# Another hand-written order for the attention stage, and the 1e-9 of the softmax sums added on another engine

## The chip, the cores and the metric

The kernel runs on one core of a Trainium2 chip. The metric is the device time of one execution in microseconds. A core has five engines that take their instructions in the order in which the program queues them, each from a queue of its own: TensorE (PE; its weight loads are PEld), VectorE (DVE), ScalarE (ACT), GpSimd (POOL) and SyncE (SP), which here only issues DMAs. They wait for each other through semaphores.

## What is computed

Causal attention over 2 batches of 12 heads (448 positions, 64 columns a head), then two mixer blocks on the 2 x 448 x 768 result. All of it is in float32 precision; weights come as 64-bit floats and are converted on the chip.

```python
def _attn_ref(q, k, v):
    scores = scale * np.matmul(q, k.transpose(0, 1, 3, 2))
    mask = np.triu(np.ones((seq, seq), dtype=bool), k=1)
    scores = np.where(mask, -1000000000.0, scores)
    scores = scores - np.max(scores, axis=-1, keepdims=True)
    attn = np.exp(scores)
    attn = attn / (np.sum(attn, axis=-1, keepdims=True) + 1e-09)
    return np.matmul(attn, v).astype(np.float32)

def _moe_ref(x, w_tok1, w_tok2, w_ch1, w_ch2):
    h = np.maximum(xt @ w_tok1, 0.0) @ w_tok2       # xt: x with positions last
    u = x + h.transpose(0, 2, 1)
    return u + np.maximum(u @ w_ch1, 0.0) @ w_ch2
...
def _moe2_ref(x, w_ch1, w_ch2):
    u = x + np.real(np.fft.fft(np.fft.fft(x, axis=1), axis=2))
    un = (u - mean(u)) / np.sqrt(var(u) + 1e-06)
    return u + np.maximum(un @ w_ch1, 0.0) @ w_ch2
```

## The kernel before

The heads are worked on in 12 pairs, n = 0 to 11, two heads side by side in TensorE's rows. The attention stage is written as a list of words, the string ORDER. A loop at the end of the stage calls one small function for each word, in the order of the list, and inside `tc.manual_schedule` this is also the order in which each engine's queue receives its instructions. So the list fixes, for every engine, what stands behind what; what can be ready when is left to the semaphores.

The words of a pair n, with the engine in brackets: Kn and Vn load q and k, and v (SyncE issues the DMAs; only the k of pair 0 is issued by ScalarE, in two halves, in `load_k`). Sn.g are the scores (TensorE), in three groups, g = 0 for the blocks of 112 and 224 columns, 1 for 336 and 2 for 448; pair 0 has four groups. Nn.i adds the mask and takes the negated maxima (VectorE, line 328, two instructions and two accumulator reads), and gives the PSUM bank of the block back. En.i is the exponential with its sum (ScalarE, line 338). Tn.u transposes the probabilities (TensorE, line 351, five groups of four), Cn.u copies them to SBUF (u = 1 and 3 on ScalarE, the others on VectorE, line 358). Pn multiplies with v (TensorE, line 371), On copies the result (ScalarE). Zn makes the divisors out of the sums: `divisors`, two instructions on VectorE, lines 385 and 386. Xn transposes back (TensorE, line 392), xn divides (VectorE, line 405), hn and gn split the result into a high and a low part (ScalarE, GpSimd).

Between them stand the words of the first mixer's start: A, B, D (TensorE) with r, s, b, d, u, w around them on ScalarE, VectorE and GpSimd; Rk loads the raw words of a weight, and Wk.0 to Wk.5 convert them (ScalarE, three times VectorE, ScalarE, GpSimd); U, Y are the first matmuls with converted weights, y, z, a what follows them. The word I0 is `tables`: an exponential on one column of a small tile, so that ScalarE's table is loaded early, and a memset of 1e-6 on VectorE over that column (lines 202 and 203).

PSUM has eight banks, given out in turn by `grab` and put back into the ring by `drop`; a word that takes a bank waits for the last reader of the bank's earlier use. SBUF tiles have few buffers too: two for v, two for each parity of pairs for q and k, two for raw weights. Behind the stage the rest of the program goes on with matmuls whose order the change doesn't touch.

Of the kernel before, what the change touches and what calls it, by code (L numbers as in the profile page):

```python
# [10 lines left out]
F32 = mybir.dt.float32  # L11
# [4 lines left out]
AF = mybir.ActivationFunctionType  # L16
ALU = mybir.AluOpType
# [4 lines left out]
TS = 112  # L22
# [48 lines left out]
ENGINES = {getattr(mybir.EngineType, e) for e in ("PE", "DVE", "Activation", "Pool", "SP")}  # L71


ORDER = """K0 I0 S0.1 S0.0 K1 S0.2 N0.1 K2 N0.0 S0.3 E0.1 N0.2 S1.0 E0.0 S1.1 N0.3 V0 K3 N1.1 E0.2 N1.0 E0.3 S1.2 T0.2 N1.2
E1.1 V1 C0.2 K4 N1.3 T0.4 T0.0 E1.0 R0 T0.1 T0.3 E1.2 C0.0 S2.1 C0.1 C0.4 S2.0 C0.3 S2.2 E1.3 P0 N2.2 Z0 N2.0
T1.1 N2.1 E2.2 E2.1 O0 T1.2 Z1 T1.0 T1.4 E2.0 N2.3 C1.2 C1.0 E2.3 C1.4 V3 X0 T1.3 x0 S3.0 S3.1 C1.1 Z2 N3.1 S3.2
W0.0 C1.3 N3.0 K5 P1 E3.0 N3.2 T2.0 E3.2 O1 E3.1 T2.2 W0.1 C2.0 T2.1 T2.3 X1 T2.4 B0.0 C2.1 C2.2 N3.3 C2.3 S4.1
b0.0 x1 S4.2 h0 C2.4 E3.3 V2 N4.2 S4.0 P2 T3.2 E4.2 T3.4 N4.3 N4.1 T3.0 W0.2 N4.0 E4.3 R1 g0 K6 W0.3 O2 V5 T3.3
E4.1 X2 T3.1 C3.0 E4.0 C3.4 x2 T4.2 C3.1 T4.0 S5.1 C3.3 C3.2 h2 N5.2 P3 W0.4 E5.2 S5.0 O3 N5.0 C4.0 C4.2 S5.2 g2
B0.2 h1 T4.4 W1.0 T4.3 W0.5 N5.1 N5.3 b0.2 T4.1 C4.1 g1 K7 A0.0 B0.1 C4.4 W1.1 A0.1 R2 V4 C4.3 Z4 E5.0 E5.3 W1.2  # L80
E5.1 Z3 r0.0 b0.1 X3 r0.1 P4 S6.0 O4 S6.1 W1.3 s0.0 W1.4 x3 T5.3 Z5 T5.2 N6.1 T5.1 s0.1 N6.0 C5.3 W1.5 T5.4 C5.2
T5.0 E6.0 C5.1 E6.1 X4 N6.2 C5.0 D0.1 K8 x4 V6 S6.2 E6.2 R3 S7.0 C5.4 W2.0 N6.3 N7.1 S7.1 h4 P5 E6.3 N7.2 V7
D0.0 B1.1 E7.2 T6.4 K9 d0.1 E7.1 O5 T6.0 W2.1 b1.1 g4 X5 T6.2 D0.2 N7.0 C6.0 C6.4 E7.0 x5 d0.0 W3.0 T6.3 T6.1 h5
C6.3 d0.2 C6.2 S7.2 S8.0 S8.1 g5 N7.3 C6.1 h3 N8.0 N8.2 S8.2 N8.1 E7.3 N8.3 g3 P6 T7.3 Z7 E8.2 E8.3 W3.1 T7.0
W2.2 B1.0 C7.3 K10 u0.2 C7.0 W2.3 T7.2 A1.1 Z6 W3.2 T7.4 T7.1 O6 E8.1 A1.0 b1.0 W2.4 B1.2 C7.1 C7.2 C7.4 X6 r1.0
P7 r1.1 s1.0 S9.2 E8.0 b1.2 S9.0 R4 s1.1 O7 x6 S9.1 u0.0 N9.3 h6 T8.4 X7 N9.2 E9.3 N9.1 V8 D1.0 E9.2 x7 V9 C8.4
T8.3 T8.0 T8.2 d1.0 C8.2 N9.0 C8.0 W3.3 K11 g6 T8.1 u1.0 C8.1 w0.2 C8.3 S10.0 u0.1 w1.0 S10.2 E9.1 N10.1 N10.3
P8 N10.0 E9.0 T9.4 T9.2 W3.4 D1.1 Z8 C9.2 O8 E10.3 T9.0 V11 w0.0 E10.1 T9.3 E10.0 D1.2 X8 h7 T9.1 C9.3 d1.1 C9.4
C9.0 d1.2 S11.2 S11.0 W2.5 x8 u1.1 h8 S10.1 N11.3 C9.1 S11.1 N11.0 E11.3 g7 N10.2 E10.2 P9 T10.1 N11.2 T10.0
N11.1 T10.3 E11.0 V10 E11.1 E11.2 C10.3 C10.0 g8 T10.2 Z9 T10.4 w1.1 C10.4 R5 Z10 A2.0 C10.2 C10.1 P10 W3.5  # L90
T11.4 w0.1 O9 T11.2 W4.0 W4.1 T11.0 T11.1 C11.4 O10 u1.2 W5.0 T11.3 W4.2 C11.3 C11.0 C11.1 A2.1 r2.0 C11.2 P11
X9 B2.1 X10 w1.2 W5.1 W4.3 B2.0 r2.1 B2.2 s2.0 s2.1 b2.1 D2.0 x9 R6 W4.4 x10 W5.2 D2.1 W5.3 O11 W4.5 W5.4 Z11 U2
y2 h10 X11 h9 D2.2 z2 b2.0 d2.1 R7 g10 W5.5 x11 d2.0 U0 W6.0 h11 W6.1 B3.0 g11 b3.0 g9 U3 A3.0 y0 y3 A3.1 r3.0
B3.2 b3.2 W6.2 z0 r3.1 s3.0 W7.0 W6.3 s3.1 U1 u2.0 W6.4 D3.1 b2.2 B3.1 D3.0 b3.1 y1 W7.1 W7.2 D3.2 W7.3 u2.1
W6.5 w2.0 W7.4 z1 z3 W7.5 d3.1 d2.2 d3.0 u3.1 w3.1 d3.2 Y0 u2.2 Y1 u3.2 w2.1 u3.0 a0 w3.0 w2.2 a1 w3.2
"""


# [5 lines left out]
def fused_kernel(ctx: ExitStack, tc: tile.TileContext, qk, v, w1, w2, wa, wb, wc, wd, fa, fb, out):  # L104
    nc = tc.nc
    mm = nc.tensor.matmul
    vec, act, pool = nc.vector, nc.scalar, nc.gpsimd

    const = ctx.enter_context(tc.tile_pool(name="const", bufs=1))
# [9 lines left out]
    vec.memset(mean_w, 1.0 / DM)  # L119
    ones = const.tile([1, 16], F32, name="ones")  # L120
    vec.memset(ones, 1.0)
    eps_t = const.tile([128, 16], F32, name="eps_t")[:, :1]

    resid = [[res.tile([128, S], F32, name=f"resid{ct}_{b}") for b in range(B)] for ct in range(NCT)]
    act_h = [[res.tile([128, S], F32R, name=f"acth{ct}_{b}") for b in range(B)] for ct in range(NCT)]
# [143 lines left out]
    with ExitStack() as actx:  # L269
        ap = actx.enter_context(tc.tile_pool(name="attn", bufs=2))  # L270
        a1 = actx.enter_context(tc.tile_pool(name="attn1", bufs=1))
# [4 lines left out]
            out=mask[:, S - TS :], in_=mask[:, S - TS :], pattern=[[-1, TS]], compare_op=ALU.is_ge, fill=MASKED,  # L276
# [105 lines left out]

        def divisors(n):
            c = pairs[n]
            vec.scalar_tensor_tensor(out=c.ssum, in0=c.ssum, scalar=1.0e-9, in1=c.ssum, op0=ALU.add, op1=ALU.max)
            vec.reciprocal(out=c.ssum, in_=c.ssum)

        def rows(n):
# [104 lines left out]
        raw, ahead, g0 = {}, [None] * (len(sources) - 2), {}  # L493
# [25 lines left out]
        def early_add(x):  # L519
# [3 lines left out]
        ops = dict(  # L523
            I=tables, K=load_k, V=load_v, S=scores, N=maxima, E=exps, T=transposes,
            C=pt_copy, P=pv, O=pv_copy, Z=divisors, X=rows, x=divide, h=x_high, g=x_low, A=mix_in, r=mix_high,
            s=mix_low, B=channels, b=channels_copy, D=mix_out, d=mix_add, u=split_high, w=split_low, R=load_raw,
            W=convert_part, U=lambda k: early_up(k, 0), y=lambda k: early_up(k, 1), z=lambda k: early_up(k, 2),
            Y=early_down, a=early_add,
        )
        with tc.manual_schedule(engines=ENGINES):  # L530
            for word in ORDER.split():
                ops[word[0]](*[int(x) for x in word[1:].split(".")])
# [274 lines left out]
    inv, rstd, g2, pools = {}, [], {}, {}  # L807
# [77 lines left out]
    with tc.manual_schedule(engines=ENGINES):  # L885
        for word in ORDER2.split():
            name = word.rstrip("0123456789.")
# [99 lines left out]
```

## Time and profile before

| | |
|---|---|
| median of 3 runs | 673.29 us (673.22 to 673.49) |
| the profiled execution | 673.2 us, of which the span is 671.4 us |
| busy share of the span | TensorE 99%, weight loads 91%, VectorE 79%, ScalarE 42%, GpSimd 17% |
| granted TensorE clock | 0.999 of full speed over the span |
| attention stage | from the start to 139.2 us |

The page gives the busy time of each engine; a matmul's end is modelled, and matmuls overlap, so a short wait of TensorE can be hidden in what is shown as busy. The chain of waits is followed back from the last instruction, and each of its pieces ends where the next one starts: there the lengths of groups of the same work can be compared. The timeline gives single instructions with their start, the windows the busy time in a stretch.

### The profile page before, as it was taken

The page shows a single profiled execution, that of the slowest core. Times are in us where ns is not written, and L with a number is a line of the kernel's source. Part 1 is how long each engine was busy: PE and PEld are TensorE (multiplying, and loading weights), DVE is VectorE, ACT ScalarE, POOL GpSimd, SP SyncE. Part 2 cuts the span into 40 slices and gives each one's busy share as a digit, 9 for nine tenths or more (in the row PEclk, how much of TensorE's full clock was granted, in tenths as well). Part 3 has the DMA queues.
Part 4 walks back from the last instruction along what each step waited for, and adds up shares of the span by engine and source line. Part 5 has one row for each costly group of instructions (what it writes and reads, how often), then busy time and mean ns, then how long its engine had stood idle before and what let it go on. Part 6 is the DMA issues. An engine that isn't in the chain of part 4 may idle for free.

```text
span 671.4 us, 10118 instructions
## 1 busy us (share of the span) xinstructions
PE 665.5 (99%) x3838; PEld 610.6 (91%) x3838; DVE 533.7 (79%) x1016; ACT 282.9 (42%) x601; POOL 111.2 (17%) x86
## 2 busy tenths in 40 slices
PE   9999999999999999999999999999999999999997
PEld 6787889999999999999999999999999999999996
DVE  7988877688988955899899869988868898556751
ACT  7989784433333333335564422224332324232200
POOL 0042343310000000400510008261002320000000
PEclk9999999999999999999999999999999999999999
DMA  7532221184352331200233232333332434222311
GB/s 230 199 133 73 106 80 63 67 253 157 136 179 95 126 109 48 95 1 1 96 113 138 97 125 94 142 99 137 105 116 102 150 142 142 82 76 76 118 42 55
DMA packets 21541, 73.77 MB, mean 110 GB/s; under 512 B 2850, under 2 KB 7714, under 8 KB 21124
## 3 DMA queue, kind: packets, MB, share of 16 engines
q1 hardware_dynamic: 20628, 69.64, 29.9%
q0 software_dynamic: 576, 3.25, 1.5%
q8 instruction: 30, 0.49, 0.3%
q10 hardware_dynamic: 288, 0.23, 0.1%
q14 instruction: 19, 0.16, 0.1%
HBM read 70.36 MB, written 2.75 MB: 109 GB/s over the span
## 4 chain that ended last, share of the span: by engine, by line
PE 96%; DVE 3%; DMA 1%; ACT 0%; SPq 0%; issue 0%
PE psum L234 13%; PE psum L236 13%; PE psum L235 13%; PE psum L255 13%; PE psum L260 13%; PE psum L259 12%; PE psum L351 4%; PE psum L315 4%; PE psum L371 3%; PE psum L441 3%; PE psum L475 2%; PE psum L746 1%; PE psum L392 1%; PE psum L461 1%; PE psum L677 1%; DMA k<-in_qk 1%
## 5 line engine op out<-in xcount | busy, mean ns | idle before, releaser
L255 PE MATMUL psum<-gh,wh 128*128 128x448 f32 x432 | 157.3, 364 | 0.0
L234 PE MATMUL psum<-acth,wh 128*128 128x448 f32 x432 | 156.8, 363 | 0.0
L236 PE MATMUL psum<-actl,wh 128*128 128x448 f32 x432 | 156.6, 363 | 0.0
L260 PE MATMUL psum<-gl,wh 128*128 128x448 f32 x432 | 156.6, 362 | 0.0
L235 PE MATMUL psum<-acth,wl 128*128 128x448 f32 x432 | 155.8, 361 | 0.0
L259 PE MATMUL psum<-gh,wl 128*128 128x448 f32 x432 | 155.7, 360 | 0.0
L142 ACT ACTIVATE m<-w 128x512 f32<-128x512 f32 (+2 forms) x92 | 70.9, 772 | 119.8 <-DVE wl L162 82.0
L160 ACT CAST wh<-m 128x512 fp32r<-128x512 f32 (+1 forms) x90 | 63.4, 704 | 92.5 <-PE psum L260 53.5
L260 PEld LDWEIGHTS psum<-gl,wh 128*128 128x128 f32 x432 | 81.1, 188 | 6.2
L236 PEld LDWEIGHTS psum<-actl,wh 128*128 128x128 f32 x432 | 81.1, 188 | 5.9
L235 PEld LDWEIGHTS psum<-acth,wl 128*128 128x128 f32 x432 | 80.9, 187 | 5.8
L259 PEld LDWEIGHTS psum<-gh,wl 128*128 128x128 f32 x432 | 80.8, 187 | 5.8 <-issue 0.2
L255 PEld LDWEIGHTS psum<-gh,wh 128*128 128x128 f32 x432 | 81.1, 188 | 4.6 <-issue 0.2
L234 PEld LDWEIGHTS psum<-acth,wh 128*128 128x128 f32 x432 | 81.0, 188 | 4.6
L149 DVE SCALAR_TENSOR_TENSOR m<-w,m 128x512 uint32<-128x512 uint32 (+2 forms) x92 | 80.2, 872 | 2.3
L162 DVE TENSOR_TENSOR wl<-m,wh 128x512 fp32r<-128x512 f32 (+1 forms) x84 | 69.4, 829 | 15.0 <-ACT wh L160 14.6
L153 DVE SCALAR_TENSOR_TENSOR m<-w,m 128x512 uint32<-128x512 uint32 (+2 forms) x92 | 79.1, 861 | 2.0
L144 DVE TENSOR_SCALAR m<-m 128x512 f32<-128x512 f32 (+2 forms) x92 | 51.0, 554 | 31.2 <-ACT m L142 30.9
L240 ACT ACTIVATE gh<-psum 128x448 fp32r<-128x448 f32 x72 | 37.8, 540 | 71.0 <-PE psum L236 70.7
L242 DVE SCALAR_TENSOR_TENSOR gl<-psum,gh 128x448 fp32r<-128x448 f32 x72 | 43.6, 618 | 30.2 <-ACT gh L240 30.2
L145 DVE TENSOR_SCALAR m<-m 128x512 uint32<-128x512 uint32 (+2 forms) x92 | 48.9, 532 | 2.4
L338 ACT ACTIVATE p<-p,small 112x224 f32<-112x224 f32 (+3 forms) x96 | 49.6, 519 | 3.0 <-DVE small L328 2.9
(144 smaller groups left out, 741.7 us busy)
## 6 DMA issues: line engine op xcount, KB each, us to landing
w<-in_wc SPq DMA_DIRECT2D x24, 768.0 KB, 4.3
w<-in_wd SPq DMA_DIRECT2D x36, 512.0 KB, 3.2
w<-in_wa SPq DMA_DIRECT2D x12, 768.0 KB, 4.4
w<-in_wb SPq DMA_DIRECT2D x18, 512.0 KB, 3.2
v<-in_v SPq DMA_DIRECT2D x12, 256.0 KB, 2.6
out<-t SPq DMA_DIRECT2D x12, 224.0 KB, 1.9
q<-in_qk SPq DMA_DIRECT2D x11, 224.0 KB, 3.8
k<-in_qk SPq DMA_DIRECT2D x11, 224.0 KB, 3.6
```

The source lines that it names most:

```text
L142: act.activation(out=m, in_=hi.bitcast(F32), func=AF.Abs)
L144: vec.tensor_scalar(out=m, in0=m, scalar1=F64_MIN, scalar2=F64_MAX, op0=ALU.max, op1=ALU.min)
L149: vec.scalar_tensor_tensor(out=mu, in0=lo, scalar=29, in1=mu, op0=ALU.logical_shift_right, op1=ALU.bitwise_or)
L153: vec.scalar_tensor_tensor(out=mu, in0=hi, scalar=0xC0000000, in1=mu, op0=ALU.bitwise_and, op1=ALU.bitwise_or)
L160: act.copy(wh, m)
L162: low_engine[0].tensor_tensor(out=wl, in0=m, in1=f(wh), op=ALU.subtract)
L234: mm(pb[:, :S], lhsT=lh, rhs=act_h[ct][b], start=ct == 0, stop=False)
L235: mm(pb[:, :S], lhsT=ll, rhs=act_h[ct][b], start=False, stop=False)
L236: tail[0] = mm(pb[:, :S], lhsT=lh, rhs=act_l[ct][b], start=False, stop=ct == NCT - 1).ins
L255: mm(pb[:, :S], lhsT=lh, rhs=gh, start=j + k == 0 and seeded is None, stop=False, skip_group_check=seeded is not None,)
L259: mm(pb[:, :S], lhsT=ll, rhs=gh, start=False, stop=False, skip_group_check=seeded is not None)
L260: tail[0] = mm(pb[:, :S], lhsT=lh, rhs=gl, start=False, stop=j == last and k == nk - 1, skip_group_check=seeded is not None,).ins
```

## The change

Three things change. The list ORDER has the same words in another order; the order within each engine's queue changes with it. The 1e-9 is added to the sums by an activation (Identity with a bias) on ScalarE, and only the reciprocal stays on VectorE. The tile that held the 1e-6 has a second column, set to 1e-9 at the start, for this bias.

Of the order, these parts are spoken of below: the beginning (I0 now stands ahead of K0, and the scores of pair 1 begin with S1.2), the loads V5, R1, V4 behind P3, and the words around S7.2 and S9.2.

```diff
-ORDER = """K0 I0 S0.1 S0.0 K1 S0.2 N0.1 K2 N0.0 S0.3 E0.1 N0.2 S1.0 E0.0 S1.1 N0.3 V0 K3 N1.1 E0.2 N1.0 E0.3 S1.2 T0.2 N1.2
-E1.1 V1 C0.2 K4 N1.3 T0.4 T0.0 E1.0 R0 T0.1 T0.3 E1.2 C0.0 S2.1 C0.1 C0.4 S2.0 C0.3 S2.2 E1.3 P0 N2.2 Z0 N2.0
...
+ORDER = """I0 K0 S0.1 S0.0 S0.2 K1 N0.1 S0.3 E0.1 N0.0 V0 N0.2 S1.2 N0.3 E0.0 S1.0 S1.1 E0.2 K2 E0.3 N1.0 N1.3 V1 T0.2 E1.3
+T0.0 T0.1 N1.1 T0.3 C0.2 T0.4 C0.1 N1.2 C0.0 R0 S2.0 C0.4 Z0 S2.1 S2.2 N2.3 C0.3 E1.2 P0 E1.1 N2.2 T1.4 N2.0 K3
...
+C3.4 Z2 C3.3 g0 X2 g1 W0.3 S5.0 E4.3 W0.4 S5.2 S5.1 P3 x2 N5.3 E4.1 N5.1 T4.4 V5 B0.1 E4.0 R1 N5.0 N5.2 B0.2 O3
+T4.2 Z3 V4 C4.2 T4.3 h2 C4.3 T4.1 X3 R2 C4.4 E5.1 T4.0 C4.1 W0.5 W1.0 g2 A0.0 r0.0 E5.2 C4.0 W1.1 E5.3 P4 s0.0
...
+T6.0 d0.0 T6.3 C6.4 T6.1 N7.1 N7.0 h4 C6.3 C6.0 C6.1 R3 K9 V6 T6.2 E7.0 X5 S7.1 S8.2 x5 g4 S8.1 N7.2 u0.0 C6.2
+S8.0 N8.2 S7.2 h5 P6 Z6 N7.3 N8.1 N8.0 K10 W3.0 g5 D0.2 E7.2 d0.1 N8.3 E7.3 E8.0 E7.1 W2.2 A1.0 B1.1 T7.2 E8.1
...
+b1.1 b1.0 X6 W3.1 P7 S9.0 V8 W3.2 x6 N9.1 r1.1 s1.1 S9.1 W2.4 O7 T8.0 Z8 N9.2 w0.1 T8.2 T8.3 W2.5 T8.1 C8.0 C8.2
+K11 R4 N9.0 w0.0 X7 E9.1 C8.3 T8.4 S9.2 E9.2 S10.0 C8.1 C8.4 N9.3 S10.2 x7 N10.1 N10.3 N10.0 E9.0 P8 E9.3 E10.1
...
-    eps_t = const.tile([128, 16], F32, name="eps_t")[:, :1]
+    eps_all = const.tile([128, 16], F32, name="eps_t")
+    eps_t, small_t = eps_all[:, :1], eps_all[:, 1:2]
+    vec.memset(small_t, 1.0e-9)
...
         def divisors(n):
             c = pairs[n]
-            vec.scalar_tensor_tensor(out=c.ssum, in0=c.ssum, scalar=1.0e-9, in1=c.ssum, op0=ALU.add, op1=ALU.max)
+            act.activation(out=c.ssum, in_=c.ssum, func=AF.Identity, bias=small_t[:TS])
             vec.reciprocal(out=c.ssum, in_=c.ssum)
```

## Rows read from the trace of the kernel before

**Rows 1.** The page: busy time of TensorE, and the chain's shares by engine.

```profile
PE 665.5 (99%) x3838; PEld 610.6 (91%) x3838; DVE 533.7 (79%) x1016; ACT 282.9 (42%) x601; POOL 111.2 (17%) x86
...
PE 96%; DVE 3%; DMA 1%; ACT 0%; SPq 0%; issue 0%
```

**Rows 2.** Waits of TensorE's matmuls, whole span: waiter, releaser, us, times, longest.

```profile
PE psum L315 <- DMA k<-in_qk: 0.6, 2, 0.4
```

**Rows 3.** The chain that ended last, attention stage: start us, us, what.

```profile
6.85 2.15 PE psum L315 x16
9.00 2.07 PE psum L351 x20
11.07 2.42 PE psum L315 x16
...
17.91 2.08 PE psum L315 x16
...
26.86 1.91 PE psum L371 x28
...
32.04 1.02 PE psum L315 x4
...
34.97 1.51 PE psum L315 x12
...
59.55 2.83 PE psum L315 x20
...
87.92 2.64 PE psum L315 x20
...
139.22 0.20 PE psum L234
```

**Rows 4.** Timeline of the start: start us, us, engine, line, operation.

```profile
0.73 0.90 ACTq L294 DMA_DIRECT2D k<-in_qk  x2
1.66 1.28 ACT L202 ACT_TABLE_LOAD   x1 [1.66 <-PEq L974]
...
7.83 0.65 ACT L338 ACTIVATE p<-p,small 112x448 f32<-112x448 f32 x1
...
8.93 2.13 PE L351 MATMUL psum<-ident,p 112*128 112x112 f32 x20
```

**Rows 5.** Two lines by themselves: duration in ns (min/median/max), first and last start.

```profile
L385 DVE SCALAR_TENSOR_TENSOR small<-small x12: 153/160/805, 13.1 to 110.6; 112x8 f32<-112x8 f32 x12
...
L837 ACT ACTIVATE r<-psum,eps_t x2: 257/260/263, 375.0 to 387.8; 112x4 f32<-112x4 f32 x2
```

**Rows 6.** Busy time in a window: us, then each engine's, clock, DMA share, GB/s.

```profile
15.00:60.00 45.00, 45.00 (x434) 36.84 (x430) 39.48 (x128) 41.28 (x126) 10.31 (x7) 1.00 0.46 153
```

**Rows 7.** Timeline of VectorE around the maxima of pair 1.

```profile
7.69 0.39 DVE L328 CUSTOM_DVE_ANT_0 p<-psum,mask 112x224 f32<-112x224 f32 x1
...
8.32 0.27 DVE L328 CUSTOM_DVE_ANT_0 p<-psum,mask 112x112 f32<-112x112 f32 x1
...
8.71 0.50 DVE L328 CUSTOM_DVE_ANT_0 p<-psum,mask 112x336 f32<-112x336 f32 x1
...
9.57 0.62 DVE L358 COPY pt<-psum 128x448 f32<-128x448 f32 x1
10.12 0.61 DVE L328 CUSTOM_DVE_ANT_0 p<-psum,mask 112x448 f32<-112x448 f32 x1
...
11.20 1.15 DVE L358 COPY pt<-psum 128x448 f32<-128x448 f32 x2
```

**Rows 8.** Two v loads as SyncE issues them; the page's medians to landing.

```profile
28.80 0.33 SPq L298 DMA_DIRECT2D v<-in_v  x1
...
35.01 0.33 SPq L298 DMA_DIRECT2D v<-in_v  x1
...
v<-in_v SPq DMA_DIRECT2D x12, 256.0 KB, 2.6
...
w<-in_w SPq DMA_DIRECT2D x2, 896.0 KB, 7.8
```

More of the change, by code (lines that the diff above doesn't have):

```diff
@@ L71 @@
 ENGINES = {getattr(mybir.EngineType, e) for e in ("PE", "DVE", "Activation", "Pool", "SP")}
-ORDER = """K0 I0 S0.1 S0.0 K1 S0.2 N0.1 K2 N0.0 S0.3 E0.1 N0.2 S1.0 E0.0 S1.1 N0.3 V0 K3 N1.1 E0.2 N1.0 E0.3 S1.2 T0.2 N1.2
-E1.1 V1 C0.2 K4 N1.3 T0.4 T0.0 E1.0 R0 T0.1 T0.3 E1.2 C0.0 S2.1 C0.1 C0.4 S2.0 C0.3 S2.2 E1.3 P0 N2.2 Z0 N2.0
-T1.1 N2.1 E2.2 E2.1 O0 T1.2 Z1 T1.0 T1.4 E2.0 N2.3 C1.2 C1.0 E2.3 C1.4 V3 X0 T1.3 x0 S3.0 S3.1 C1.1 Z2 N3.1 S3.2
-W0.0 C1.3 N3.0 K5 P1 E3.0 N3.2 T2.0 E3.2 O1 E3.1 T2.2 W0.1 C2.0 T2.1 T2.3 X1 T2.4 B0.0 C2.1 C2.2 N3.3 C2.3 S4.1
@@ L78 @@
[L78 to L92, printed above, removed]
@@ L93 @@
-y2 h10 X11 h9 D2.2 z2 b2.0 d2.1 R7 g10 W5.5 x11 d2.0 U0 W6.0 h11 W6.1 B3.0 g11 b3.0 g9 U3 A3.0 y0 y3 A3.1 r3.0
-B3.2 b3.2 W6.2 z0 r3.1 s3.0 W7.0 W6.3 s3.1 U1 u2.0 W6.4 D3.1 b2.2 B3.1 D3.0 b3.1 y1 W7.1 W7.2 D3.2 W7.3 u2.1
-W6.5 w2.0 W7.4 z1 z3 W7.5 d3.1 d2.2 d3.0 u3.1 w3.1 d3.2 Y0 u2.2 Y1 u3.2 w2.1 u3.0 a0 w3.0 w2.2 a1 w3.2
+ORDER = """I0 K0 S0.1 S0.0 S0.2 K1 N0.1 S0.3 E0.1 N0.0 V0 N0.2 S1.2 N0.3 E0.0 S1.0 S1.1 E0.2 K2 E0.3 N1.0 N1.3 V1 T0.2 E1.3
+T0.0 T0.1 N1.1 T0.3 C0.2 T0.4 C0.1 N1.2 C0.0 R0 S2.0 C0.4 Z0 S2.1 S2.2 N2.3 C0.3 E1.2 P0 E1.1 N2.2 T1.4 N2.0 K3
@@ new lines @@
+N2.1 E1.0 T1.2 T1.3 C1.2 W0.0 O0 T1.0 T1.1 X0 E2.1 C1.1 E2.3 C1.4 S3.0 C1.0 S3.2 x0 K4 N3.1 C1.3 W0.1 N3.0 E2.2
+V3 S3.1 P1 E2.0 B0.0 O1 N3.3 T2.2 T2.3 Z1 T2.4 T2.1 b0.0 T2.0 C2.2 N3.2 C2.4 E3.1 X1 E3.0 C2.3 S4.0 C2.1 C2.0 V2
+K5 x1 E3.2 S4.2 S4.1 N4.3 E3.3 P2 W0.2 T3.1 T3.2 K6 h0 O2 N4.2 h1 T3.0 E4.2 N4.1 C3.2 N4.0 T3.3 T3.4 C3.0 C3.1
+C3.4 Z2 C3.3 g0 X2 g1 W0.3 S5.0 E4.3 W0.4 S5.2 S5.1 P3 x2 N5.3 E4.1 N5.1 T4.4 V5 B0.1 E4.0 R1 N5.0 N5.2 B0.2 O3
+T4.2 Z3 V4 C4.2 T4.3 h2 C4.3 T4.1 X3 R2 C4.4 E5.1 T4.0 C4.1 W0.5 W1.0 g2 A0.0 r0.0 E5.2 C4.0 W1.1 E5.3 P4 s0.0
@@ new lines @@
+E5.0 W1.2 K7 A0.1 T5.2 x3 T5.3 O4 C5.2 b0.2 X4 b0.1 T5.0 C5.3 T5.1 T5.4 W1.3 r0.1 s0.1 S6.1 h3 W1.4 C5.0 W1.5
+C5.4 S6.2 C5.1 N6.2 Z5 g3 E6.2 K8 N6.3 S6.0 Z4 S7.0 W2.0 N6.1 N6.0 P5 E6.3 D0.0 E6.0 x4 T6.4 E6.1 W2.1 O5 D0.1
+T6.0 d0.0 T6.3 C6.4 T6.1 N7.1 N7.0 h4 C6.3 C6.0 C6.1 R3 K9 V6 T6.2 E7.0 X5 S7.1 S8.2 x5 g4 S8.1 N7.2 u0.0 C6.2
+S8.0 N8.2 S7.2 h5 P6 Z6 N7.3 N8.1 N8.0 K10 W3.0 g5 D0.2 E7.2 d0.1 N8.3 E7.3 E8.0 E7.1 W2.2 A1.0 B1.1 T7.2 E8.1
+d0.2 r1.0 T7.1 s1.0 T7.3 E8.2 C7.2 C7.3 W2.3 T7.4 B1.2 Z7 b1.2 T7.0 C7.0 C7.4 C7.1 A1.1 V7 u0.1 O6 E8.3 B1.0
@@ new lines @@
+b1.1 b1.0 X6 W3.1 P7 S9.0 V8 W3.2 x6 N9.1 r1.1 s1.1 S9.1 W2.4 O7 T8.0 Z8 N9.2 w0.1 T8.2 T8.3 W2.5 T8.1 C8.0 C8.2
+K11 R4 N9.0 w0.0 X7 E9.1 C8.3 T8.4 S9.2 E9.2 S10.0 C8.1 C8.4 N9.3 S10.2 x7 N10.1 N10.3 N10.0 E9.0 P8 E9.3 E10.1
+T9.0 h6 T9.4 T9.2 T9.1 W4.0 D1.1 O8 h7 C9.4 C9.0 W3.3 T9.3 X8 W3.4 E10.3 D1.0 S10.1 x8 C9.2 d1.1 C9.3 S11.0
+S11.1 N10.2 g7 N11.1 C9.1 S11.2 E10.0 V9 N11.0 E10.2 P9 N11.3 E11.0 h8 T10.0 d1.0 u0.2 g6 T10.3 T10.2 T10.1 R5
+W3.5 E11.1 g8 T10.4 V11 W4.1 C10.0 C10.1 N11.2 C10.4 C10.3 u1.1 A2.0 V10 C10.2 W4.2 P10 E11.2 W4.3 E11.3 W5.0
@@ new lines @@
+T11.3 T11.2 W5.1 u1.0 T11.1 W4.4 O9 D1.2 C11.1 Z10 T11.0 W4.5 w0.2 C11.2 T11.4 C11.0 A2.1 d1.2 r2.0 w1.1 C11.3
+u1.2 C11.4 P11 B2.1 R6 r2.1 Z9 Z11 s2.1 O10 B2.0 s2.0 W5.2 X10 X9 W6.0 B2.2 W6.1 W5.3 D2.0 w1.0 b2.2 x9 h9 O11
+W5.4 D2.2 b2.1 W6.2 x10 w1.2 U2 h10 b2.0 g9 X11 x11 d2.2 D2.1 B3.1 B3.2 d2.0 y2 W6.3 R7 h11 u2.0 g10 d2.1 B3.0
+U0 g11 W5.5 W6.4 A3.1 w2.0 A3.0 U3 u2.1 y0 r3.0 b3.0 z0 r3.1 W7.0 b3.1 s3.1 W7.1 b3.2 y3 s3.0 D3.2 u2.2 z3 U1 y1
+D3.1 z2 D3.0 W7.2 d3.2 W7.3 W7.4 z1 d3.1 d3.0 u3.2 w2.1 w3.2 u3.0 w3.0 W6.5 W7.5 Y0 u3.1 a0 w3.1 Y1 w2.2 a1
```

## The prediction

> **What bounds the kernel now.** The span is 671.4 us, and the profiled execution took 673.2 us, so 1.8 us lie around the span; the median of the three runs is 673.29 us, 0.1 us above the profiled one. Terms below are added to 673.2. I read the page first: TensorE is busy 99% of the span, and 96% of the chain that ended last is TensorE work [rows 1]. Then the waits of TensorE over the whole span: it waited for the first loads, and behind those for nothing that the view shows [rows 2]. Then the chain in order of time through the attention stage: it enters TensorE at 6.85 us, when the keys of pair 1 have landed (pairs count from 0), and from there each piece begins where the one before it ends [rows 3]. Those pieces are TensorE's up to the handover to the next stage at 139.2 us, and behind it TensorE goes on as densely [rows 1, 3]. So a microsecond more or less of TensorE time in the attention stage is one of the whole kernel, and time on the other engines is worth nothing until TensorE waits for it. Only three things can move the end: the 6.85 us before the dense part, the switches between kinds of matmuls, and waits.
>
> The waits are partly hidden in pieces that the view calls busy. A pair's scores in one run of words (S words) take 2.08 us; those of pair 2 take 2.42, so 0.34 us of waiting sit in them [rows 3]. The scores of pair 5 are cut in two around another word and take 1.02 and 1.51 us, 0.45 us over 2.08 [rows 3].
>
> **The change part by part.** *The start.* SyncE issues q and k of pairs 0 and 1 in the same order as before, and the chain up to 6.85 us hangs on them alone [rows 3]. The V load that now follows them was issued later before; it stands behind them in the queue, so it takes nothing from them. I take 0 for this. New is that the table load and the eps write (word I0) stand ahead of K0 on ScalarE, and K0 issues the first keys from ScalarE's queue. Today ScalarE issues the two DMAs from 0.73 to 1.63 us, and the table load follows at 1.66 and takes 1.28 us [rows 4]; the small activation behind it is put at 0.25, from the nearest row of 0.26 [rows 5]. If ScalarE's queue hands the DMAs on while the table load runs, they are some 0.1 us late; if not, they are 1.28 + 0.25 = 1.5 us late. Behind them hang the first scores, the maxima, the exponentials and the first transposes. The exponential that those need ended at 8.48 us, and they started at 8.93, when TensorE came free [rows 4]: 0.44 us of slack. So the end moves by 0 at one bound and 1.5 - 0.44 = 1.06 us at the other, a little more if the late keys also share the DMA engines with those of pair 1. No row shows ScalarE issuing a DMA behind compute. I take 0, the bound that lies nearer to the one handover of this queue that is shown (0.03 us from the second DMA to the table load [rows 4]); the other bound is the first rival.
>
> The Trainium skill has a page for this ("Perfetto Trace Analysis", the section on DVE and Act engine instructions): the sequencer pushes an instruction into a wait queue and is then free to decode the next. By that rule the DMAs are not held and the start costs 0; no row here shows it for a table load.
>
> *The 1e-9.* VectorE loses 12 instructions of 0.16 us (median) on 112x8 elements [rows 5], some 2 to 2.7 us in all. ScalarE gains 12 activations with a bias tile on the same 8 columns. The nearest rows are VectorE's own 0.16 us and an activation of 112x4 with a bias tile on ScalarE, 0.26 us [rows 5]; between them I take 0.25, as it is the same engine and form, so 3 us in all. One more memset, of the bias column, lies before any input has landed. None of it is on the path; its cover is ScalarE's idle time, 45.0 - 41.28 = 3.7 us from 15 to 60 us [rows 6], where about six of the twelve fall, 1.5 us. That is thin but enough. The change adds a wait: the reciprocal on VectorE now waits for ScalarE, and behind it in VectorE's queue stand maxima, whose end gives PSUM banks back to the next S words. In the new order VectorE has 1 to 3 other steps between the last exponential and the reciprocal in most pairs, so I take 0, with an upper end of 0.25 us for each of the three or four pairs in ScalarE's fullest stretch, 1 us.
>
> No row shows this function (Identity). The Trainium skill ("ScalarE: Activation LUTs", the section on table sets) says that cheap functions such as copy, relu and identity are in every table set. Copies, Relu and Abs run between the exponentials here without a load between them, and the page's rule says the same of the new one.
>
> *Switches.* Counted in the two orders, S words behind the first block stand in 11 runs before and 9 after: pair 5 is no longer cut, and pairs 6 to 11 come in 5 runs in place of 6. Price of a cut: the eight runs of pairs 5 to 11 take 15.01 us (from 1.02 at 32.04 us to 2.64 at 87.92; the others are 1.51, 1.33, 2.08, 2.83, 2.08 and 1.52) [rows 3], against 7 x 2.08 = 14.56 in seven runs: 0.45 for one cut, of which I put 0.25 down to a wait in pair 5, so 0.2 us. Two cuts fewer are worth 0.4 us (0.9 if all of the 0.45 were the cut). The other switches (transposes, P, X, A, B, D, U) change places but not much in number. Term: -0.4 us.
>
> *Waits that go.* The two that sit in pairs 2 and 5: 0.34 + 0.25, -0.6 us, if the new order has none in their place.
>
> *Waits that come.* (1) The scores of pair 1 now begin with the block of 448 columns (S1.2). By its share of columns it takes 0.86 of the 2.15 us, and the next word, S1.0, 0.65 [rows 3]; so VectorE, which is done with the maxima of pair 0 at 7.69 us [rows 7] and begins pair 1 with N1.0, waits until 6.85 + 0.86 + 0.65 = 8.4 us for something to read. Then come three maxima words, 0.39 + 1.08 + 0.63 us, and the copy of 0.6 us that returns a bank [rows 7]: 8.4 + 2.1 + 0.6 = 11.1 us, and TensorE wants the bank at 11.07 (9.00 + 2.07) [rows 3]. This is the wait that pair 2 has today, about as large: +0.3. (2) Near 59 us the block S7.2 was moved behind S8.2, S8.1 and S8.0 and takes a bank of S8.2. Between the end of S7.1 and this, TensorE has some 2.0 us of scores (three of the four words of a 2.83 us run [rows 3]); VectorE has N7.2, C6.2 and N8.2, two maxima words of 0.86 us and a copy of 0.55, 2.3 us and a handover [rows 7]. +0.3. (3) Near 77 us S9.2 stands behind five transpose groups and a copy of the same kind; the sums differ by less than 0.2, so 0 to 0.3, and I take +0.3, since a late bank also costs the overlap of the two heads in a block: 0.34 us today. Of shorter ones that I don't see I add +0.2.
>
> *Transfers.* The loads of v, q, k and raw weights stand in another order on SyncE. The tightest: V5 and V4 both come after P3 now, with the first 0.9 MB weight load (R1) between them. Today V5 is issued at 28.80 us and V4 at 35.01 [rows 8], just behind P2 and P3, which end at 28.77 and 34.97 [rows 3]; so each takes the buffer freed earliest in the order, and V5 will again wait for P2 only, and V4 for P3, with R1 far ahead. P4 comes behind P3, five transpose groups (2.07 us [rows 3]), a mixing word of twelve matmuls and three transposing words, and a v load lands in 2.6 us [rows 8]. I take 0; if V5 took P3's buffer, V4 would stand behind R1, which takes up to 7.8 us to land [rows 8], and P4 would wait some 3 us.
>
> Sum: -0.4 - 0.6 + 0.3 + 0.3 + 0.3 + 0.2 = +0.1 us; 673.2 + 0.1 = 673.3 us.
>
> **The rivals.** (a) *ScalarE's DMAs are held behind the table load.* For it: the trace shows the reverse order kept strictly, the table load waited for the DMAs to be issued [rows 4], so the queue is in order. Against it: in order needn't mean finished, and no row shows which. Price 1.06 us, and up to 0.5 more for the shared DMA engines; it decides as soon as the keys are over 0.44 us late. 1.3 more: 674.6 us. (b) *Waits on the bound side:* the reciprocals hold VectorE (1 us), or V4 comes late (up to 3 us): 675.2 us with 2 us as the middle. For it: ScalarE at 92% and VectorE at 88% busy from 15 to 60 us [rows 6]; against it: TensorE gets through the same stretch today with 0.6 us of waiting. (c) *The new order has no waits and the cuts are worth 0.9:* 673.2 - 0.6 - 0.9 = 671.7 us. For it: VectorE is lighter by over 2 us; against it: the sums at 11 us and 59 us.
>
> **How the numbers follow.** The forecast, 673.3 (672.3 to 674.2), has 0.70; (a) 0.17; (b) 0.06; (c) 0.07. A measurement of this kernel can tell about 0.2%, 1.35 us, from no change: below 671.95 or above 674.65. Half of (a) and all of (b) lie above it, most of (c) below: faster 0.06, same 0.80, slower 0.14. The range reaches into (a) and leaves out (b) and most of (c): 672.2 to 674.8.
>
> **What would show it.** In the profile after: the two DMA issues on ScalarE before 1 us show the start right, at 2.2 us they show (a), with the first transposes at 10 us in place of 8.93. S runs of 2.08 us in the chain show no waits; those near 11, 59 and 77 us should read up to 0.3 us more. The handover to the next stage (139.2 us today) gives the sum of all terms. The forecast is wrong if that handover moves by over 1.3 us, or if anything behind it moves, which the change doesn't touch.

## The result, and the profile after

| | before | after |
|---|---|---|
| median | 673.38 us of 6 runs (673.22 to 673.79) | 678.40 us of 6 runs (678.01 to 678.59) |
| ratio | | 1.0074 (95% interval 1.0063 to 1.0084) |
| span of the profiled execution | 671.4 us | 676.5 us |

The changed kernel is slower by 5.0 us, 0.74%. The forecast was 673.3 us, with 674.8 as the upper end of the range. In code and profile of the changed kernel, lines below 122 of the file are moved down by two: the L315 of before is L317, L142 is L144, L489 is L491.

First the page (busy time of TensorE, shares of the chain), and all waits of TensorE behind 2 us (waiter, releaser: us, times, longest), which answer to [rows 1] and [rows 2]:

```profile
PE 667.2 (99%) x3838; PEld 612.7 (91%) x3838; DVE 532.5 (79%) x1005; ACT 286.1 (42%) x613; POOL 110.5 (16%) x86
...
PE 92%; DVE 4%; DMA 2%; issue 0%; ACT 0%; SPq 0%; ACTq 0%; DVEq 0%
```

```profile
PE psum L238 <- DVE actl L491: 2.7, 1, 2.7
PE psum L317 <- DMA k<-in_qk: 1.3, 2, 1.1
PE psum L443 <- DVE pt L360: 0.5, 1, 0.5
```

A new wait of 2.7 us stands in it, on a low half (line 491, a w word: what the high half of a value leaves over), and the chain now runs for 8% of the span through other engines than TensorE. The chain in order of time (start us, us, what) tells where; its attention part answers to [rows 3]:

```profile
2.12 4.86 DMA k<-in_qk
...
7.12 2.15 PE psum L317 x16
...
11.33 2.54 PE psum L317 x12
...
57.15 3.74 PE psum L317 x24
...
77.70 2.51 PE psum L317 x13
...
91.46 1.56 DVE m L146
...
93.52 0.63 DVE pt L360
...
94.29 2.33 PE psum L443 x12
...
131.16 0.69 DVE m L155
...
131.91 8.69 DMA w<-in_wb
...
140.68 0.09 ACT m L144
...
141.25 0.56 ACT acth L487
...
141.83 0.62 DVE actl L491
142.46 0.60 DVE m L151
143.06 0.54 DVE resid L269
143.60 1.08 DVE actl L491 x2
...
144.72 0.74 PE psum L238
145.46 0.37 PE psum L236
...
147.70 0.27 PE psum L236
147.97 0.20 PE psum L237
```

From 131.91 us on this view has the loss behind the attention stage in a column. A weight of the next stage (512 KB) is issued and lands 8.69 us later. ScalarE's conversion of it (line 144) stands ahead of two casts of the attention stage (line 487), these ahead of three low halves on VectorE (line 491), and a matmul needs the last of those at 144.72. Then TensorE's matmuls follow each other at 0.37 us in place of 0.20. The windows show why (us, busy of PE, PEld, DVE, ACT and POOL, granted clock, DMA share, GB/s):

```profile
140.00:142.00 2.00, 2.00 (x11) 1.53 (x9) 0.17 (x1) 1.32 (x3) 0.00 (x0) 1.00 0.01 2
142.00:144.00 2.00, 0.00 (x1) 0.00 (x0) 2.00 (x4) 0.27 (x1) 0.00 (x0) 1.00 0.00 0
144.00:146.00 2.00, 1.28 (x3) 1.16 (x4) 2.00 (x5) 0.00 (x0) 0.00 (x0) 0.58 0.00 0
146.00:148.00 2.00, 2.00 (x7) 1.81 (x6) 1.90 (x4) 0.00 (x0) 0.00 (x0) 0.57 0.74 262
148.00:150.00 2.00, 2.00 (x11) 1.87 (x10) 1.06 (x3) 1.05 (x2) 0.00 (x0) 1.00 0.46 143
```

After the idle time the clock is at its lower level (1.2 GHz of 2.4) until near 148 us. The eight matmuls from 144.72 to 147.97 us take 3.25 us, against 8 x 0.20 = 1.60: 1.65 us more.

Why did the load take 8.69 us? GpSimd's timeline of the changed kernel, then that of the kernel before (start us, us, what, and in brackets the idle time ahead and its releaser):

```profile
125.34 0.72 POOL L582 DMA_DIRECT2D fah<-in_fa  x1 [4.41 <-issue]
126.05 0.57 POOL L582 DMA_DIRECT2D fal<-in_fa  x1
126.59 0.62 POOL L582 DMA_DIRECT2D fbh<-in_fb  x1
127.19 0.54 POOL L582 DMA_DIRECT2D fbl<-in_fb  x1
```

```profile
132.59 0.71 POOL L580 DMA_DIRECT2D fah<-in_fa  x1 [1.52 <-PE psum L461]
...
135.28 0.58 POOL L580 DMA_DIRECT2D fal<-in_fa  x1
```

These four loads bring the constants of a much later stage, 3.2 MB, into memory that the attention tiles give up. Before, the last reader of those tiles was B3.1 (the transposes of line 461, 131.6 to 132.0 us), and the loads went out behind the weight load that is issued at 131.70. In the new order the B3 words are done by 117 us. The profile names no releaser for the loads there; by the times it is A3.0, whose matmuls end at 124.72 us, 0.62 us ahead of the first load, as B3.1 ended 0.62 us ahead of it before. So the loads are in flight when the weight load goes out. The DMA issues from 124 to 142 us (KB each, median us to landing), before and after:

```profile
w<-in_wb SPq DMA_DIRECT2D x2, 512.0 KB, 3.1
```

```profile
w<-in_wb SPq DMA_DIRECT2D x1, 512.0 KB, 8.7
...
fbl<-in_fb POOLq DMA_DIRECT2D x1, 409.6 KB, 13.2
```

The weight was issued 4.7 us after the last of the four and landed 0.2 us after it (131.91 + 8.69 = 140.60; 127.19 + 13.2 = 140.4).

The account of the 5.1 us of span, with the handover to the next stage read in both timelines as the first matmul of the up-projections behind Y1, 139.06 us before and 140.24 after: +1.18 us up to there; +4.38 from there to the last matmul of the kernel (527.62 and 532.00 us), of which 2.71 are the wait and 1.65 the lower clock; and -0.43 for what follows the last matmul (4.74 and 4.31 us). This last part can't be put down to the change: the early reader in the old order (below) has 4.28 us there too, and all other runs have 4.27 to 4.31.

### The profile page after: what moved, and what is told of

It is laid out like the page before. It is cut to its first block, busy times and chain, and to the rows that moved or that the text cites. A ratio compares the mean times of both kernels' runs of the same rounds, so it can differ in the third digit from the quotient of the medians.

```text
span 676.5 us, 10145 instructions
## 1 busy us (share of the span) xinstructions
PE 667.2 (99%) x3838; PEld 612.7 (91%) x3838; DVE 532.5 (79%) x1005; ACT 286.1 (42%) x613; POOL 110.5 (16%) x86
## 3 DMA queue, kind: packets, MB, share of 16 engines
q0 software_dynamic: 576, 3.25, 1.6%
## 4 chain that ended last, share of the span: by engine, by line
PE 92%; DVE 4%; DMA 2%; issue 0%; ACT 0%; SPq 0%; ACTq 0%; DVEq 0%
PE psum L238 13%; PE psum L236 13%; PE psum L237 13%; PE psum L257 12%; PE psum L262 12%; PE psum L261 12%; PE psum L317 3%; PE psum L353 3%; PE psum L373 3%; PE psum L443 3%; PE psum L477 2%; DMA w<-in_wb 1%; PE psum L748 1%; PE psum L394 1%; PE psum L463 1%; DMA k<-in_qk 1%
## 5 line engine op out<-in xcount | busy, mean ns | idle before, releaser
L144 ACT ACTIVATE m<-w 128x512 f32<-128x512 f32 (+2 forms) x92 | 70.9, 772 | 120.2 <-DVE wl L164 86.4
L155 DVE SCALAR_TENSOR_TENSOR m<-w,m 128x512 uint32<-128x512 uint32 (+2 forms) x92 | 78.9, 858 | 1.9
L151 DVE SCALAR_TENSOR_TENSOR m<-w,m 128x512 uint32<-128x512 uint32 (+2 forms) x92 | 78.5, 854 | 2.2
```

What stands on the lines that cost most here:

```text
L144: act.activation(out=m, in_=hi.bitcast(F32), func=AF.Abs)
L151: vec.scalar_tensor_tensor(out=mu, in0=lo, scalar=29, in1=mu, op0=ALU.logical_shift_right, op1=ALU.bitwise_or)
L155: vec.scalar_tensor_tensor(out=mu, in0=hi, scalar=0xC0000000, in1=mu, op0=ALU.bitwise_and, op1=ALU.bitwise_or)
```

## The experiments

Theory 1: GpSimd's loads go out early, stretch the weight load, and its conversion holds casts and low halves that TensorE needs. Rival 2: the queues at the end of the list are in a bad order whatever the loads do. Rival 3: the addition on ScalarE is what costs. The median of the kernel before beside these runs was 673.33 to 673.35 us.

**The reader late.** One pair of words is moved back.

```diff
-... d2.2 D2.1 B3.1 B3.2 d2.0 ... W7.0 b3.1 s3.1 ... D3.1 z2 D3.0 W7.2 ...
+... d2.2 D2.1 B3.2 d2.0 ... W7.0 s3.1 ... D3.1 z2 B3.1 D3.0 b3.1 W7.2 ...
```

> The changed order with one pair of words moved back: B3.1, the last reading of the attention rows that stood at the end in the old order, goes behind D3.1 again, its copy b3.1 behind D3.0. Theory 1 (GpSimd's four constant loads): the four loads, 3.2 MB, go out when the last reader of the attention tiles is done; in the old order that was B3.1 at 131.7 us and they went out at 132.59 and from 135.28, in the new one at 125.34 to 127.19, and the weight load issued at 131.91 then took 8.69 us in place of 3.05. With B3.1 late the loads go out at about 132 again, the weight load lands by about 135, TensorE's wait of 2.71 us near 142 and the stretch at the lower clock behind it go: 678.4 - 4 = 674.4 us (673.9 to 674.9); what is left over the kernel before, about 1 us, was lost before 140 us. Rival 2 (the queues at the end of the list: two casts stand behind a conversion in ScalarE's queue, and three low halves behind them in VectorE's, whatever the load does): nothing of that is moved here, so the wait stays and the time is 678 or above.

Measured: 676.28 us (675.54 to 679.23), ratio 1.0053 (1.0038 to 1.0067). The weight load issued at 131.62 landed in 3.2 us, and the wait near 142 us is gone, against rival 2. But the four loads now went out from 135.09 to 138.18 us, later than before, and the next weight load, issued at 140.99, met them: 8.7 us again (149.71). TensorE paid 20 us later (its timeline):

```profile
161.19 0.47 PE L262 MATMUL psum<-gl,wh 128*128 128x448 f32 x1 [1.60 <-DVE gl L244]
```

```profile
163.00:166.00 3.00, 3.00 (x17) 2.81 (x16) 2.86 (x6) 1.04 (x2) 0.00 (x0) 1.00 0.54 199
```

The mechanism held, and the expected time did not. Behind the handover 1.33 us were lost in this execution (528.95 us to the last matmul in place of 527.62), since the loads met another weight; the handover itself was 0.72 us later than in the changed kernel (140.96 against 140.24), and where that comes from was not followed up. Here the wait was 1.60 us and the clock stayed at 1.00 (second fence, the window from 163 to 166 us; columns as above).

**A load held.** The list as changed; a copy of one element ahead of the loads reads what d3.1 writes.

```diff
+    pool.tensor_copy(fah[0:1, 0, 0:1], resid[4][1][0:1, 0:1])
     for t, src in ((fah, fa[0]), (fal, fa[1]), (fbh, fb[0]), (fbl, fb[1])):
         pool.dma_start(out=t, in_=src)
```

> The changed kernel with its order as it is; one copy of a single element stands ahead of GpSimd's four constant loads and reads the tile that d3.1 writes (135.27 us in the changed kernel), so that the loads go out at about 135.5 instead of 125.34. Theory 1: the weight load issued at 131.91 lands by about 135, the wait of 2.71 us and the lower clock go, 674.4 us (673.9 to 674.9), the same as with the late reader. Rival 2 (the queues at the end of the list): 678.4 us. A third outcome, in which the loads come too late for what needs them, would show as a wait far behind 200 us; the kernel before has them land at 138.7 to 145.7 without one, so about 137 to 148 should be early enough.

Measured: 674.01 us (673.30 to 674.14), ratio 1.0007 (0.9998 to 1.0015). The copy held one load only: fal, fbh and fbl still went out from 124.70 to 125.94 us, fah at 135.87. With 1.2 MB less ahead of it the weight load took 5.3 us (131.27 to 136.56), TensorE waited for nothing behind the handover, and 4.4 us came back. Not all of the loads have to move.

**The early reader in the old order.**

```diff
-... A3.1 r3.0 B3.2 b3.2 ... b2.2 B3.1 D3.0 b3.1 y1 ...
+... A3.1 r3.0 B3.1 B3.2 b3.1 b3.2 ... b2.2 D3.0 y1 ...
```

> The kernel before with B3.1 and b3.1 moved forward, next to B3.2 and b3.2: nothing else of the change. Theory 1: GpSimd's loads go out at about 127 to 129 us in place of 132.59 and 135.28, the weight load issued at 131.70 lands near 140 in place of 134.75, the conversion of ScalarE waits for it, and TensorE waits 1 to 3 us near 141 and loses about 1.3 us more at the lower clock: 673.4 + 2 to 4 = 675.4 to 677.4 us. Rival 2 (the queues at the end of the changed list, not the loads): 673.4 us, within 0.3.

Measured: 674.44 us (673.92 to 680.12, twelve runs), ratio 1.0029 (1.0014 to 1.0044). In the right direction, but the median is below what was expected: GpSimd had other work between the loads, which went out at 128.06, 131.67, 134.36 and 134.91 us; the weight load took 6.3 us, and in the profiled execution (673.99 us) TensorE waited 0.2 us. That was one of the quick ones. Four of the twelve took 676.23 to 680.12 us, and the two longest have a mean clock of 0.997 and 0.995, as the changed kernel has (0.996 to 0.997); what they waited for no trace shows. The early reader alone brings a part of the loss. That the part hangs on how the loads lie against the weight load is likely and not shown.

**The order alone, the addition alone.** In the first, the list is the changed one and `divisors` that of before; in the second it is the other way round.

> The changed order, with the 1e-9 added by VectorE as before. Theory 1 puts the whole loss down to the order: 678.0 to 678.8 us, the weight load again takes over 8 us. Rival 3 (the addition on ScalarE holds up VectorE or ScalarE and costs a part of it): below 677.5, and up to 673.4 if all of it.

> The old order with the 1e-9 added on ScalarE: the other half of the change by itself. If the addition costs nothing, as the prediction put it: 673.3 us, within 0.3. If the reciprocal's wait for ScalarE holds VectorE up in the old order: 673.6 to 674.4. The changed order with the addition left on VectorE took 679.31, 0.9 us more than with it on ScalarE; if that 0.9 is what 12 fewer instructions on VectorE are worth in any order, this run should show 672.4 to 673.0.

Measured: the order alone 679.31 us (677.85 to 679.54), ratio 1.0084 (1.0071 to 1.0097); the weight load took 8.5 us. That is above what was expected; rival 3 falls for the changed order, where the addition on ScalarE shows no cost (678.40 against 679.31, with intervals of the ratio that overlap). The addition alone, in the old order: 675.37 us (675.35 to 675.57), ratio 1.0030 (1.0018 to 1.0041), 2.0 us slower, which none of its expectations held. VectorE's waits from 10 to 25 us in that run, and the chain there:

```profile
DVE small L388 <- ACT small L387: 2.2, 2, 1.5
```

```profile
16.72 0.42 ACT ots L382
17.14 0.21 ACT small L387
...
17.37 0.04 DVE small L388
17.41 0.08 issue
17.49 0.49 DVE p L330
...
18.67 3.20 PE psum L317 x12
```

The addition for pair 1 stands behind four exponentials of pair 2 and a copy in ScalarE's queue, the reciprocal waits 1.5 us for it, behind that the maxima, and for the banks that these give back the scores of pair 3. The product with v of pair 1 begins at 21.80 us, 1.89 later than in the kernel before, of which 0.30 stood there since the start. Between the products of pairs 4 and 5 go another 0.6 us (9.63 in place of 9.04), where a reciprocal waits 1.93 us. In the changed kernel three reciprocals wait too, up to 1.5 us, and no matmul waits for them. So the price of the addition is set by the list: in the old one 2.0 us, in the new one none that can be told.

**The casts first.** The conversion of the late weight goes behind the stage's last cast; list and loads stay.

```diff
...
-            act.copy(act_h[ct][b], resid[ct][b])
+            last_high[0] = act.copy(act_h[ct][b], resid[ct][b]).ins
...
-    early_low = last_low[0]
+    early_low = [last_low[0], last_high[0]]
...
-        hold[:] = [early_low]
+        hold[:] = early_low
```

> The changed kernel with its order and with the four constant loads where they are; only the conversion of the weight that lands late is put behind the last cast of the attention stage (a second instruction to issue after). The weight load should again take over 8 us. If the loss behind the handover is that the late weight's conversion stands in ScalarE's and VectorE's queues ahead of casts and low halves that TensorE needs at 142 us: the wait of 2.71 us and the lower clock go although the load is as late as before, 674.0 to 674.8 us, since the weight itself is first used some 14 us later. If TensorE needed the late weight itself soon, or the casts are late for another reason: 677 us or more.

Measured: 673.87 us (673.53 to 674.42), ratio 1.0008 (0.9999 to 1.0016). ScalarE's timeline:

```profile
136.25 1.04 ACT L487 CAST acth<-resid 128x448 fp32r<-128x448 f32 x2 [0.44 <-DVE resid L482]
137.19 0.67 ACT L144 ACTIVATE m<-w 128x512 f32<-128x512 f32 x1
141.00 0.66 ACT L144 ACTIVATE m<-w 128x512 f32<-128x512 f32 x1 [3.14 <-DMA w<-in_wb]
```

The load was as late as ever (9.0 us, 131.88 to 140.92) and ScalarE still waited 3.14 us for it, but with nothing needed soon behind it: no wait of TensorE behind the handover, granted clock 1.00 from 140 to 150 us, 4.5 us back. So the late load costs only because its conversion stands ahead of the casts: theory 1 needs the queue of rival 2 for its last step, and rival 2 the late load, since without it (load held, loads spread) the same queue costs nothing.

**The loads spread.** Eight pieces of some 0.4 MB, each held behind an up-projection of the next two blocks.

```diff
+            if bulk:
+                next_bulk(f(g[fm, 1][1]))
...
-    for t, src in ((fah, fa[0]), (fal, fa[1]), (fbh, fb[0]), (fbl, fb[1])):
-        pool.dma_start(out=t, in_=src)
+    bulk = [(t[:, i], src[:, i]) for t, src in ((fah, fa[0]), (fal, fa[1])) for i in range(3)]
+    bulk += [(fbh, fb[0]), (fbl, fb[1])]
+    def next_bulk(late):
+        t, src = bulk.pop(0)
+        one = (slice(0, 1),) + (0,) * (len(t.shape) - 2) + (slice(0, 1),)
+        pool.tensor_copy(t[one], late[0:1, 0:1])
+        pool.dma_start(out=t, in_=src)
```

> The changed kernel with its order as it is; the 3.2 MB of constants go out in eight pieces of about 0.4 MB, each held behind one of the next two blocks' up-projections (a copy of one element that reads a low half just made). No bulk transfer then runs near 131 us, nor near the two weight loads behind it. Theory 1 (the bulk transfers stretch the weight load): 673.8 to 674.6 us, weight loads near 131, 141 and 144 us at 3 to 3.5 us each, and no wait of TensorE behind the handover. If a piece stretches the weight load that runs beside it by more than the two raw buffers cover, there would be new waits of TensorE behind 200 us, and up to 676.

Measured: 674.16 us (673.57 to 674.41), ratio 1.0010 (1.0001 to 1.0019); the three weight loads took 3.0 to 3.3 us and TensorE waited for nothing behind the handover. In all three, held load, casts first and spread loads, the last matmul starts 527.6 us behind the handover, as in the kernel before.

**The start as before,** on top of the casts first: K0 ahead of I0, K2 ahead of V0, S1.2 last.

> The same as the run with the casts first, and the start of the list as in the old order: K0 ahead of I0, K2 ahead of V0, S1.0 and S1.1 ahead of S1.2. The profiled starts of the changed order so far (first matmuls of P0 at 13.13 to 13.91 us, 13.42 in the kernel before) hang on when the keys of pair 1 land. If the start of the list costs the 0.3 us by which it was late in the changed kernel: 0.3 us less than the run with the casts first. If that was only the spread of the landing: the same within 0.3.

Measured: 674.09 us (673.35 to 675.32), ratio 1.0008 (0.9999 to 1.0017), against 673.87: the same. The first matmul of P0 came at 15.17 us in its profiled execution, the longest of the eleven, and at 13.13 to 13.91 in the others. Not the keys of pair 1 alone set this, as the expectation had it: here the chain goes through the second half of pair 0's keys, which had landed at 4.94 us, and the scores of pair 1 end at 10.43 us, in eight other profiles at 8.58 to 9.36. The start spreads, why it does is open, and the start of the list shows no cost that these runs can tell.

**The conversion behind the copies,** on top of the casts first.

```diff
-... g8 T10.4 V11 W4.1 C10.0 C10.1 N11.2 C10.4 C10.3 u1.1 A2.0 V10 C10.2 W4.2 ...
+... g8 T10.4 V11 C10.0 C10.1 N11.2 C10.4 C10.3 u1.1 A2.0 V10 C10.2 W4.1 W4.2 ...
```

> The run with the casts first, and in the list the word W4.1 (two instructions of VectorE that convert a weight) moved from ahead of C10.0 to behind C10.2. In the changed kernel these two took 2.1 us from 91.38, the first of them 1.63 us beside a subtraction of GpSimd from 91.31 to 92.60, and the copy of C10.0 behind them, which gives the bank back that A2.0 takes, ended at 94.1; TensorE waited 0.46 us and A2.0 took 2.33 us instead of 2.11. If that is the loss between P9 and P10: the distance of the two starts falls from 6.76 to about 6.1 us, and the time from 673.87 to 673.2 (673.0 to 673.6). If the copy is late for another reason (the maxima of pair 11 ahead of it end at 90.9, and 20 transposes only at 93.8): less than 0.3 us are won and the wait stays.

Measured: 673.15 us (672.62 to 674.39), ratio 0.9997 (0.9988 to 1.0006): 0.72 us less than without it, though the intervals of the two ratios overlap. The trace is the clearer witness: from the start of P9 to that of P10 it is 6.09 us in place of 6.76. (In the profiled execution the start was 0.66 us earlier besides, and 0.55 us were lost near 158 us, where matmuls followed each other at 0.31 to 0.39 us.) GpSimd's subtraction and VectorE's conversion in the timelines of the changed kernel, then of this one, and A2.0 in the chain of this one:

```profile
91.31 1.29 POOL L430 TENSOR_TENSOR xl<-x,xh 112x512 fp32r<-112x512 f32 x1 [2.04 <-ACT xh L424]
91.38 1.63 DVE L146 TENSOR_SCALAR m<-m 128x768 f32<-128x768 f32 x1
```

```profile
90.65 1.28 POOL L430 TENSOR_TENSOR xl<-x,xh 112x512 fp32r<-112x512 f32 x1 [2.05 <-ACT xh L424]
94.26 0.55 DVE L146 TENSOR_SCALAR m<-m 128x768 f32<-128x768 f32 x1
```

```profile
93.15 2.11 PE psum L443 x12
```

With this the changed list is level with the kernel before, and no version here beats it by more than can be told. The run shows that the place of the conversion costs; that GpSimd's subtraction made it long rests on the times of the two alone.

## Why the prediction was wrong

The step that failed is that on transfers, and with it the sentence that the handover "gives the sum of all terms". It followed SyncE's queue and its buffers, and of "anything behind it" it said "which the change doesn't touch". By its own last sentence the forecast is wrong through this part, not through the handover, which moved by 1.18 us. Two things reach over the handover: what the attention tiles' last readers release (GpSimd's loads wait for that, in a queue that the step did not look at), and the conversions of the next stage's weights, which stand among the last words in ScalarE's and VectorE's queues. Measured: 2.71 us of waiting and 1.65 us at the lower clock, 4.36 of the 4.38 us lost there. That both the late load and the queue are needed is shown by the held load and by the casts first; the term had been 0.

The steps up to the handover, in their order:

- *The start.* Right in its mechanism. ScalarE's timeline has the table load and, while it runs, the two issues of the keys:

```profile
0.73 1.28 ACT L204 ACT_TABLE_LOAD   x1 [0.73 <-PEq L976]
0.80 0.86 ACTq L296 DMA_DIRECT2D k<-in_qk  x2
```

  So rival (a) is out: the queue handed the DMAs on 0.07 us into the table load. The Trainium skill ("Perfetto Trace Analysis", the section on DVE and Act engine instructions) says that the sequencer can decode the next instruction once it has pushed one into the wait queue; the trace agrees. Pair 1's scores began 0.27 us later than in [rows 3], with the keys landing 4.86 us after their issue in place of 4.60. That is within the spread of the profiled starts, and the start as before did not win it back.
- *The 1e-9.* The activation takes 0.30 us (median of 12), 0.25 was put. That a reciprocal can hold VectorE was rival (b) with 1 us of its price; in the new order it did not decide (waits of up to 1.5 us, for which no matmul waited), in the old one the addition costs 2.0 us. No new table load came.
- *Switches and waits of the scores.* The runs of S words behind the first block add up to 21.59 us in the chain before and 21.75 after (2.54, 2.08 three times, 2.67, 3.74, 1.33, 2.51, and 2.72 from 87.07 to P9 at 89.79): +0.16, where the terms -0.4 - 0.6 + 0.3 + 0.3 + 0.3 make -0.1. Pair 5, no longer cut, took a clean 2.08. The three waits that were priced at 0.3 each came out at 0.46, 0.2 and 0.2 us: pair 2 at 11 us took 2.54 against 2.08 clean; the run near 57 us (S7.1, pair 8, S7.2) has 1904 columns, a pair has 1120, so by their share it would take an estimated 3.54 and took 3.74; that at 77.70 (S9.2, S10.0, S10.2: 1232 columns) 2.29 and took 2.51.
- *Between P9 and P10:* +0.68 us, 6.76 against 6.08. In the sum only the "shorter ones that I don't see", put at +0.2, stand for it. The last run shows the cause: a conversion of 1.63 us stood ahead of a copy that gives a bank back.
- *V5 and V4:* right, no matmul waited for them.

Start 0.27, scores 0.16 and this 0.68 make 1.11 of the 1.18 us. The loss up to the handover alone would have been inside the range (673.2 + 1.2 = 674.4 us); what left it lay behind.

## What to carry to other kernels

When an order changes, list what each tile's last reader releases, on every queue, and ask which transfer the released one will run beside. A hand-over time is not the end of the change: follow the in-order queues past it, and put whatever waits for a transfer behind what the busiest engine needs next. A sum that stops at the hand-over, like the one here, sees neither.

## What the chip showed that was not expected

- A 512 KB load issued by SyncE beside GpSimd's 3.2 MB landed only with the last of these, in 8.5 to 9.1 us in place of 3.1, in the runs where all four were ahead of it (at most 0.4 us before the last, at most 0.2 after). The Trainium skill ("DMA: Bandwidth & Descriptors", the rules for kernel authors) says that loads issued by different engines run on the same 16 DMA engines and interleave. The sharing agrees with the trace, the interleaving only late: in the changed kernel GpSimd's queue moved 169 packets from 131.9 to 134 us and SyncE's none, then SyncE's moved 12 of the load's 144 until 136 us and 90 until 138. In the kernel before, with nothing ahead of it, 137 of them went from 131.7 to 134.2 us.
- VectorE's conversion of 128x768 took 1.63 us beside a GpSimd subtraction, and 0.55 without. The Trainium skill ("SBUF — State Buffer", who interferes with whom) says that VectorE in its two-port mode, which a tensor_scalar like this one can enter, shares a port pair with GpSimd, and that the first to issue holds it for the whole instruction while the other is blocked. The trace agrees roughly: the conversion began 0.07 us after GpSimd's 1.29 us and ended 0.41 us behind it; alone it takes 0.55.
- In the changed kernel the granted clock was at 0.58 behind 2.71 us without matmuls; with the late reader it stayed at 1.00 behind 1.60 us.
